# A fused transformer block: start, modulation, softmax helpers and the hand-over to the feed-forward rearranged

## The chip, the cores and the metric

The kernel runs on one core of a Trainium2 chip. The metric is the device time of one execution in microseconds (us), median of several runs; lower is better. The names of the engines in the profile are PE (TensorE, matrix multiplication), PEld (its weight loads), DVE (VectorE), ACT (ScalarE), POOL (GpSimd) and SP (SyncE, which issues most transfers here). A profile's span is about 1.7 us shorter than the time of the same run (493.4 against 495.09 us before).

## The reference

The input has 2048 tokens of 576 features, 32 heads of 18, and a feed-forward of 4608. Cut to what matters:

```python
mod = (silu(c) @ w_mod)             # six vectors of 576: sa, ca, ga, sb, cb, gb
h = layernorm(x) * (1 + ca) + sa
q, k, v = h @ wqkv
phi(q) = [softmax(q w_phi), softmax(-q w_phi)]    # per head; the same for k
kv = sum over tokens of phi(k) v ;  z = sum of phi(k)
x = x + ga * ((phi(q) kv / (phi(q) z)) @ wo)
h = layernorm(x) * (1 + cb) + sb
x = x + gb * (relu(h @ w1) @ w2)
```

`kv` sums over all tokens, so the whole key and value pass must end before the first attention output. That gives the kernel three parts: the key/value loop over 16 tiles of 128 tokens, a transition (two tiles of attention output must be ready before the feed-forward can start), and the feed-forward in five blocks, with the other 14 tiles' attention output interleaved.

## The kernel before

The parts that the argument touches. Instructions of the loop are placed by a scheduler from data dependences and priorities; in the last part PE's order is that of the program.

```python
# start: one transfer per weight; fold W_k with w_phi; the 60 one-column modulation matmuls
load_rows(nc.sync, wk_raw, A_wqkv[:, D:2 * D], False)
...
def mod_columns(parts, dst):                 # 2 x 30 matmuls whose moving operand has ONE column
    ps = one()
    ...     nc.tensor.matmul(ps[p0:p0 + pn, n * NC + ci:n * NC + ci + 1],
                             lhsT=wmod_sb[i][0:k, ck, ci * P:ci * P + pn], rhs=siluc[0:k, ck:ck + 1], ...)

def k_softmax(t):                            # one half on GpSimd, the other on DVE
    nc.vector.tensor_reduce(out=R[:, 0, :], in_=E, axis=AXX, op=ALU.add)
    nc.scalar.activation(out=R[:, 0, :], in_=R[:, 0, :], func=ACT.Ln)
    nc.scalar.activation(out=R[:, 1, :], in_=R[:, 0, :], func=ACT.Exp, scale=-1.0)
    for sgn, eng in ((1, nc.gpsimd), (0, nc.vector)):
        e = E[:, sgn * H:(sgn + 1) * H, :]
        eng.tensor_tensor(out=e, in0=e, in1=R[...].to_broadcast([P, H, DH]), op=ALU.mult)

def a_filler(t):                             # extra work of loop step t
    if t == 0: fold_transposes(wq_raw, wqT, "a")
    if t == 1: fold(wqT, wq_sb, "a")
    if t == 3:
        nc.gpsimd.tensor_copy(rep[:], ...)
        mod_row(2, ga_row)                   # a row: 10 matmuls of 288 columns
    if t == 5:
        mod_row(5, gb_row); mod_columns((3, 4), mod2)
    if 7 <= t < 13: q_part(...)              # query pieces
    if t == 14:
        for ci in range(NC):
            nc.gpsimd.tensor_tensor(out=wo_sb[:, ci, :], in0=wo_sb[:, ci, :], in1=ga_row[:], op=ALU.mult)

# transition
num_tile(0); q_part(3, 0); q_part(3, 1); num_tile(1); tr_tile(0); q_part(3, 2)
wo_tile(0); tr_tile(1); wo_tile(1); feat(0, ...)   # then the feed-forward's first block
```

`num_tile` is numerator, denominator and their quotient; its last step adds two halves (`o_sb`) on GpSimd. `tr_tile` transposes it, `wo_tile` is the output projection with the residual and the second norm.

The softmax here doesn't subtract the row's maximum and nothing guards it: scores larger than these inputs give would overflow.

## Time and profile before

| stage of the profiled run | from to (us) | length |
|---|---|---|
| start, to the end of the first key tile | 0 to 27.1 | 27.1 |
| loop, to the end of the last kv tile | 27.1 to 120.1 | 93.0 |
| kv to kvzd (the masked kv) | 120.1 to 121.9 | 1.8 |
| transition | 121.9 to 142.6 | 20.7 |
| feed-forward, first block | 142.6 to 199.0 | 56.4 |
| feed-forward, the rest | 199.0 to 493.4 | 294.4 |

Median time 493.17 us. The table by stage of the kernel before: stretch in us, its length, busy us (and instructions) of each engine, PE's granted clock as a share, DMA share and GB/s.

```profile
27.10:53.00 25.90, 24.19 (x221) 15.93 (x219) 21.70 (x49) 21.29 (x57) 9.75 (x7) 0.93 0.09 29
53.00:119.40 66.40, 63.26 (x515) 39.57 (x514) 29.85 (x33) 43.83 (x103) 21.46 (x15) 0.92 0.29 102
121.90:142.60 20.70, 13.67 (x89) 7.64 (x89) 10.50 (x32) 8.77 (x25) 2.80 (x2) 0.80 0.22 78
142.60:198.90 56.30, 53.09 (x455) 36.91 (x454) 29.24 (x89) 15.49 (x46) 5.64 (x4) 0.95 0.09 27
198.90:449.70 250.80, 250.68 (x1726) 146.63 (x1724) 108.76 (x261) 52.56 (x120) 14.34 (x10) 1.00 0.02 8
```

From 198.9 to 449.7 us PE is busy 250.68 of 250.8 us, at a granted clock of 1.00. In front of that, the last rows show where it is not: in the transition PE works 13.67 of 20.7 us, at a mean clock of 0.80.

The waits of PE in the kernel before: who waited for whom, us in total, times, longest.

```profile
PE two L230 <- DMA rW<-in_A_wqkv_dram: 6.2, 1, 6.2
PE pt L512 <- POOL o_sb L506: 5.9, 4, 2.7
...
PE two L206 <- ACT rH L309: 2.7, 1, 2.7
PE two L230 <- DVE rW L237: 1.7, 1, 1.7
```

The first line is the start: PE waits for the key weights. `pt L512 <- POOL o_sb` is a tile's transposes waiting for the GpSimd addition, 2.7 us in the transition and 3.2 us in the first block. The third line is the loop's one long gap. The timeline of PE around it (start, us, engine, line, operation, operands, count, idle time in front and what ended it):

```profile
58.76 2.66 PE L206 MATMUL two<-rW,rep 128*128 128x288 bf16 x10 [2.75 <-ACT rH L309]
61.36 3.73 PE L195 MATMUL one<-siluc,rW 128*128 128x1 bf16 x50
65.01 2.10 PE L294 MATMUL two<-rW,rH 128*128 128x288 bf16 x8
...
67.40 2.06 PE L294 MATMUL two<-rW,rH 128*128 128x252 bf16 x8
```

Eight matmuls of 288 columns take 2.10 us there, 0.26 us each; at full clock they take 1.15 us. So the gap is followed by about 10 us near half speed: the granted clock was 0.52 from 58.76 to 68.0 us, where it was 1.00 from 35 to 58. What DVE and GpSimd did just ahead of the gap, two timelines of the kernel before:

```profile
49.01 6.91 POOL L409 TENSOR_TENSOR wo_sb<-wo_sb,ga_row 128x576 bf16<-128x576 bf16 x5
```

```profile
49.58 1.23 DVE L262 SCALAR_TENSOR_TENSOR rs<-mv,rs 128x2 f32<-128x2 f32 x1
50.73 5.35 DVE L266 TENSOR_SCALAR xn<-x_sb,rs 128x576 bf16<-128x576 bf16 x4
56.00 1.34 DVE L323 TENSOR_REDUCE R_sb<-rH 128x64 f32<-128x1152 bf16 x1
```

The scaling of `wo_sb` was written for step 14 of the loop, but nothing held it there, and the scheduler put it where GpSimd was free. DVE's normalisations (L266), about 0.4 us each otherwise, take 1.34 us each on average meanwhile, and the tiny instruction at 49.58 takes 1.23 us. The softmax of the tile behind them (L323) starts late.

### The profile page before, as it was taken

How to read it: one execution, taken by the hardware profiler on the slowest of the kernel's cores; microseconds unless marked ns; L12 is line 12 of the kernel's file. 1: busy time of each engine (PE TensorE's matmuls, PEld its weight loads, DVE VectorE, ACT ScalarE, POOL GpSimd, SP SyncE). 2: the span in 40 equal slices, each digit the busy share in tenths (PEclk: the TensorE clock that was granted, in tenths of full speed). 3: DMA queues.
4: the chain of work that ended last, by engine and by line, in shares of the span. 5: the costliest groups of instructions: out<-in, count | busy, mean ns of one | idle time of the engine just before them, and what ended most of it. 6: DMA issues, size and time to landing. Idle time of an engine off the chain costs nothing.

```text
span 493.4 us, 8203 instructions
## 1 busy us (share of the span) xinstructions
PE 464.2 (94%) x3490; PEld 289.8 (59%) x3490; DVE 227.9 (46%) x544; ACT 160.4 (33%) x391; POOL 59.5 (12%) x67
## 2 busy tenths in 40 slices
PE   3999799999679889999999999999999999999996
PEld 3756476565346567433677743467773337777674
DVE  5378833435545754233565432356443332453321
ACT  3369447886523312123211222321112220112300
POOL 4013622233201120000112000011100000110000
PEclk9989869999959999999999999999999999999999
DMA  8940065007200300000000000000000000000000
GB/s 256 362 129 1 1 248 185 1 1 241 84 1 1 108 1 13 13 0 0 2 14 13 13 12 1 0 1 14 13 12 13 0 1 2 23 14 13 1 1 25
DMA packets 17263, 22.67 MB, mean 46 GB/s; under 512 B 1994, under 2 KB 16586, under 8 KB 16714
## 3 DMA queue, kind: packets, MB, share of 16 engines
q1 hardware_dynamic: 16016, 22.12, 13.1%
q8 instruction: 27, 0.44, 0.4%
q10 hardware_dynamic: 1210, 0.02, 0.1%
q14 instruction: 10, 0.08, 0.1%
HBM read 19.78 MB, written 2.36 MB: 45 GB/s over the span
## 4 chain that ended last, share of the span: by engine, by line
PE 84%; DVE 6%; ACT 5%; POOL 1%; DMA 1%; issue 1%; SPq 0%; POOLq 0%; DVEq 0%; ACTq 0%
PE psf L569 29%; PE psf L549 25%; PE two L294 6%; PE psf L553 5%; PE psf L294 3%; PE num L469 2%; PE two L361 2%; PE one L195 2%; PE kvacc L337 1%; PE two L298 1%; POOL o_sb L506 1%; DMA x_sb<-in_A_x_dram 1%; PE pt L512 1%; ACT rH L285 1%; ACT rH L309 1%; PE psf L277 1%
## 5 line engine op out<-in xcount | busy, mean ns | idle before, releaser
L549 PE MATMUL psf<-h2T,rW 128*128 128x512 bf16 (+1 forms) x720 | 142.6, 341 | 0.0
L569 PEld LDWEIGHTS <-rH 128*128 128x128 bf16 x1152 | 109.8, 98 | 28.9 <-issue 0.7
L569 PE MATMUL psf<-rW,rH 128*128 128x288 bf16 x864 | 115.1, 286 | 0.0
L549 PEld LDWEIGHTS <-rW 128*128 128x128 bf16 x720 | 64.1, 99 | 57.3 <-issue 12.0
L559 DVE TENSOR_SCALAR rH<-psf 128x512 bf16<-128x512 f32 (+1 forms) x90 | 52.5, 583 | 97.2 <-PE psf L553 97.0
L557 ACT ACTIVATE rH<-psf 128x512 bf16<-128x512 f32 (+1 forms) x90 | 46.1, 512 | 129.7 <-PE psf L553 129.7
L506 POOL TENSOR_TENSOR o_sb<-rV 128x576 bf16<-128x576 f32 x16 | 22.8, 1424 | 296.2 <-DVE rV L502 296.2
L572 DVE TENSOR_TENSOR yt<-psf,gb_row 128x288 f32<-128x288 f32 x32 | 14.6, 455 | 63.7 <-PE psf L569 63.7
L294 PE MATMUL two<-rW,rH 128*128 128x288 bf16 (+2 forms) x256 | 43.0, 313 | 1.0 <-DVE rH L288 0.8
L569 PE MATMUL psf<-rEQ,rH 128*128 128x288 bf16 x288 | 40.5, 286 | 0.0
L323 DVE TENSOR_REDUCE R_sb<-rH 128x64 f32<-128x1152 bf16 x16 | 21.6, 1352 | 25.9 <-ACT rH L309 25.9
L328 POOL TENSOR_TENSOR rH<-rH,R_sb 128x576 bf16<-128x576 bf16 x16 | 24.3, 1521 | 74.7 <-ACT R_sb L325 66.9
L553 PE MATMUL psf<-h2T,rW 64*128 64x512 bf16 (+1 forms) x180 | 31.5, 346 | 0.0
L294 PEld LDWEIGHTS <-rH 128*128 128x128 bf16 x256 | 24.2, 104 | 11.7 <-issue 2.2
L515 ACT ACTIVATE oT<-pt 128x640 bf16<-128x640 bf16 x16 | 11.3, 709 | 57.5 <-PE pt L514 57.5
L553 PEld LDWEIGHTS <-rW 64*128 64x128 bf16 x180 | 8.6, 93 | 30.9 <-issue 30.9
L256 DVE BATCH_NORM_STATS2 st<-x_sb 128x6 f32<-128x288 bf16 x64 | 25.6, 438 | 2.2 <-DMA x_sb<-in_A_x_dram 2.2
L522 DVE TENSOR_TENSOR x_sb<-x_sb,psf 128x288 bf16<-128x288 bf16 x32 | 13.2, 450 | 22.4 <-PE psf L298 22.4
L309 ACT ACTIVATE rH<-two 128x576 bf16<-128x576 f32 x32 | 19.2, 657 | 8.6 <-PE two L298 8.5
L294 PE MATMUL psf<-wo_sb,oT 128*128 128x288 bf16 x128 | 19.3, 296 | 1.4 <-ACT oT L515 1.4
L266 DVE TENSOR_SCALAR xn<-x_sb,rs 128x576 bf16<-128x576 bf16 x32 | 16.7, 546 | 1.4 <-PE one L280 1.2
L260 ACT ACTIVATE rs<-mv,eps_t 128x1 f32<-128x1 f32 (+2 forms) x24 | 7.0, 297 | 31.7 <-DVE mv L257 31.7
(99 smaller groups left out, 407.1 us busy)
## 6 DMA issues: line engine op xcount, KB each, us to landing
rW<-in_B_w_dram SPq DMA_DIRECT2D x1, 4608.0 KB, 14.1
rW<-in_B_w_dram SPq DMA_DIRECT2D x3, 1296.0 KB, 9.4
rW<-in_w_mod_dram SPq DMA_DIRECT2D x6, 576.0 KB, 7.5
out_dram<-x_sb SPq DMA_DIRECT2D x16, 144.0 KB, 1.7
rW<-in_A_wqkv_dram SPq DMA_DIRECT2D x3, 576.0 KB, 5.3
rEQ<-in_B_w_dram SPq DMA_DIRECT2D x1, 1296.0 KB, 6.1
x_sb<-in_A_x_dram SPq DMA_DIRECT2D x1, 1152.0 KB, 10.7
x_sb<-in_A_x_dram SPq DMA_DIRECT2D x1, 576.0 KB, 6.6
```

Source lines behind the costliest of these rows:

```text
L256: nc.vector.bn_stats(out=s[:, hf, :], in_=x_sb[:, t, hf * HD2:(hf + 1) * HD2])
L266: nc.vector.tensor_scalar(out=xn[:, t % NX, :], in0=x_sb[:, t, :], scalar1=rs[:, n, t, 0:1], scalar2=rs[:, n, t, 1:2], op0=ALU.mult, op1=A ...
L294: nc.tensor.matmul(ps(bk)[:, 0:cn], lhsT=lhs(ci, 0, P), rhs=rhs[:, ci, c0:c0 + cn], start=(ci == 0), stop=False)
L309: nc.scalar.activation(out=E[:, sgn, :].rearrange("p (b f) -> p b f", b=2), in_=ps[:, :, 0:HD2], func=ACT.Exp, scale=1.0 - 2.0 * sgn)
L323: nc.vector.tensor_reduce(out=R[:, 0, :], in_=E, axis=AXX, op=ALU.add)
L328: eng.tensor_tensor(out=e, in0=e, in1=R[:, 1, sgn * H:(sgn + 1) * H].unsqueeze(2).to_broadcast([P, H, DH]), op=ALU.mult)
L506: nc.gpsimd.tensor_tensor(out=o_sb[:, t % NO, :], in0=tm[:, 0, :], in1=tm[:, 1, :], op=ALU.add)
L549: nc.tensor.matmul(hps[n][:, 0:nn], lhsT=w1a[:, ci, jj * P:(jj + 1) * P], rhs=h2T[:, ci, 0:nn], start=(ci == 0), stop=False)
L553: nc.tensor.matmul(hps[n][:, 0:nn], lhsT=w1b[b0:b0 + 64, j * P:(j + 1) * P], rhs=h2T[b0:b0 + 64, 4, 0:nn], start=False, stop=True)
L557: nc.scalar.activation(out=H1[:, jj, 0:nn], in_=hps[n][:, 0:nn], func=ACT.Relu)
L559: nc.vector.tensor_relu(H1[:, jj, 0:nn], hps[n][:, 0:nn])
L569: nc.tensor.matmul(ps[:, 0:cn], lhsT=H1[:, j, tt * P:(tt + 1) * P], rhs=w2q[j // 9][:, j % 9, c0:c0 + cn], start=(j == 0), stop=(j == NJ - 1))
```

## The change

The intent: use idle time of PE before the feed-forward, take waits out of the loop and the transition, and keep PE's clock up. The diff, cut to its core (helpers split into a matmul part and an evacuation part, memory moves, the order of later loads, the copy `rep` moved from GpSimd to DVE and a few evacuations moved between ACT and DVE are left out):

```diff
 # start
+    for k in range(NC):                        # five transfers instead of two
+        nc.sync.dma_start(wk_raw[0:n, k, :], A_wqkv[k * P:k * P + n, D:2 * D])
+    order.enter_context(tc.manual_schedule(engines=ALL3))   # PE, ACT, DVE in program order
+    warm = one()
+    for i in range(24):
+        nc.tensor.matmul(warm[:, 0:P], lhsT=ident[:, :], rhs=ident[:, :], start=True, stop=True)
     ...  fold before mod_columns((0, 1)); transposes chunk by chunk over all groups;
     ...  the first features in three PSUM banks instead of one
 # loop
-    softmax: Ln, Exp on ACT
+    if t < 5: Ln, Exp on ACT
+    else:     nc.vector.reciprocal(out=R[:, 1, :], in_=R[:, 0, :])
-    t == 5:  mod_row(5, gb_row); mod_columns((3, 4), mod2)
-    t == 14: wo_sb scaled on GpSimd
+    11 <= t < 16: wo_sb scaled on DVE
+    query pieces at t = 4, 5, 7, 8, 9, 11, 12, 13, 15
 # transition, in fixed order on PE, ACT and DVE, with two 3-bank PSUM buffers
+    modulation 3 and 4 as rows plus 12 one-column matmuls, 5 as a row, between the steps
+    first two tiles: the final addition on DVE; the residual added on PE (identity matmul)
+    wo_x_stats(0, xps[0]); ln_rstd(1, 0, 1); tr_mm(1, trp); tr_e(1, trp); ln_apply(1, 0) ...
 # feed-forward
-    a tile's steps every 5 slots
+    a tile's steps 6.5 us (first block) or 7.5 us apart; transposes 6.6 us after the numerator
```

## The prediction

> **What bounds the kernel now.** From 199 us on TensorE is busy 100% at full granted clock (table by stage): the feed-forward, whose matmuls the change leaves alone. Only the first 199 us can give anything. The timeline shows four losses there:
>
> - *Start.* TensorE waits 6.2 us for the key weights, then 1.7 us for a DVE copy queued behind layer-norm statistics (waits of PE). The first key tile ends at 27.1 us.
> - *Half-speed TensorE.* 288-column matmuls take 0.26 us each at 25 and 65 us, 0.13 later.[...] it is slow before 35 us, at 58.8 to 69.4 and at 142.6 to 148, each time after gaps or one-column matmuls.
> - *45 to 70 us.* GpSimd scales wo_sb for 6.91 us from 49.0; meanwhile four DVE normalisations take 5.35 us instead of about 1.5. The softmax behind them is late, PE idles 2.75 us at 56, then runs cold through a modulation row (2.66 us), 50 one-column modulation matmuls (3.7) and tile 6.[...]
> - *119 to 199 us.* kvzd is ready at 121.9, the feed-forward starts at 142.6: a serial chain over two tiles, PE busy 6.2 of the last 12.7 us. The first block then takes 56.4 us for some 51 of warm work: cold start about 2.6, waits for o_sb 3.2.
>
> **What the change does.**
>
> 1. Key weights arrive in five pieces, 24 dummy matmuls run before, order on PE, ACT, DVE is fixed, the fold precedes the modulation columns. First key tile ends near 21 us: 6 us gained.
> 2. Then to the last kv tile: warm work, summed from durations at 105 to 113 us (k and v 2.64 per tile, kv 0.6, query pieces 2.2/2.2/1.3, features 1.4 per block, folds 4, one row 1.3), is 77 us, plus 2.3 for an early query piece; I add 3 for cold clock, 4 for stalls: it ends near 107.5 (120.1 before). Wo scaling and a softmax reciprocal (estimate 0.56 us per tile, from 0.38 for 35 elements and 0.19 for 5) load DVE nearly like PE up to tile 11, but the GpSimd collision and 22 small ACT steps go.
> 3. The second norm's modulation becomes rows plus 12 tiny matmuls that fill gaps of the transition. kvzd to feed-forward: 20.7 to 18 us; its chain stays serial. The add moves from GpSimd (1.41) to DVE[...].
> 4. First block: warm clock, wider spacing: 56.4 to 52 us.
> 5. The rest, 294 us, unchanged. The second weight's load now waits into the transition; 3.9 MB took about 11 us, over 20 remain before use: no cost.
>
> Sum: 109 + 18 + 52 + 294 = **473 us**, range 465 to 481. Chances: faster by over 2% (below 483.3) 0.95, within 2% 0.045, slower 0.005. Start gives 6, loop 7, transition 3, first block 4.
>
> **Signs.** Right if: first key tile ends near 21 us; DVE normalisations stay near 0.4 us; no 2.7 us PE gap; feed-forward starts near 127 us with 0.13 us matmuls; no waits for o_sb in the first block.
>
> **What would make it wrong.** DVE as new bound in tiles 1 to 11 (PE waiting for DVE); TensorE cold for long after the 60 one-column matmuls at the start; the fixed ACT order in the transition, where the second tile's copy stands behind the first tile's square root; feed-forward weights late (PE waiting on a DMA).

## The result

The changed kernel took 478.02 us (median of 9 runs, 477.43 to 480.58), the kernel before 493.23 us (median of 15). The ratio is 0.9691, 95% interval 0.9672 to 0.971. All ratios here are the mean time of one kernel's fast runs over that of the other's fast runs of the same rounds, so not quite the ratio of the medians. All kernels below gave correct results.

| stage | before | predicted | after (profile) |
|---|---|---|---|
| start | 27.1 | 21 | 22.2 |
| loop | 93.0 | 86.5 | 89.6 |
| kv to kvzd | 1.8 | 1.5 | 1.8 |
| transition | 20.7 | 18 | 18.75 |
| first block | 56.4 | 52 | 51.5 |
| rest | 294.4 | 294 | 292.4 |
| span | 493.4 | 473 | 476.3 |

The prediction took its sum of stages for the time; the time is 1.75 us more than the span (478.05 for the profiled run).

The table by stage of the changed kernel, with its own stage borders:

```profile
22.20:53.00 30.80, 25.18 (x220) 15.94 (x220) 27.84 (x65) 19.41 (x55) 5.40 (x5) 0.94 0.37 102
53.00:111.60 58.60, 57.27 (x465) 35.41 (x464) 35.89 (x44) 40.44 (x81) 18.12 (x12) 1.00 0.23 86
113.60:132.30 18.70, 15.63 (x115) 8.53 (x116) 10.04 (x28) 9.74 (x29) 0.00 (x0) 0.91 0.02 2
132.30:183.90 51.60, 50.56 (x453) 36.30 (x453) 31.18 (x90) 15.20 (x45) 5.61 (x4) 1.00 0.32 107
183.90:433.40 249.50, 249.50 (x1726) 147.04 (x1724) 111.89 (x261) 52.53 (x120) 14.03 (x10) 1.00 0.02 8
```

The first stretch of the loop (22.2 to 53, the value of tile 0 to the start of tile 5) has PE busy only 25.18 of 30.8 us; the second 57.27 of 58.6. The first block runs at full clock with 1 us idle. The waits of PE in the changed kernel, the longest:

```profile
PE kvacc L373 <- DVE rH L364: 2.1, 4, 0.9
...
PE two L271 <- ACT rH L275: 1.6, 1, 1.6
PE n L327 <- ACT oT L608: 1.5, 1, 1.5
PE two L271 <- ACT rW L261: 0.9, 1, 0.9
```

The old long waits are gone, for the transfer, for `o_sb` in the feed-forward and for the tile after the gap. In their place stand PE waiting for DVE's softmax multiplication (L364), for ACT's copies of the folded weights (L271), and for the copy of the second tile in the transition (`n L327 <- ACT oT`). The timeline of PE at that last wait:

```profile
122.18 1.15 PE L327 MATMUL n<-wo_sb,oT 128*128 128x288 bf16 x8
...
126.48 1.76 PE L327 MATMUL n<-wo_sb,oT 128*128 128x288 bf16 x8 [1.50 <-ACT oT L608]
...
128.53 2.45 PE L219 MATMUL n<-rW,rep 128*128 128x288 bf16 x10
...
132.78 1.16 PE L665 MATMUL psf<-h2T,rW 128*128 128x256 bf16 x7 [0.18 <-DVE h2T L318]
```

The same projection takes 1.15 us for the first tile and 1.76 us for the second, after the wait; the row behind it takes 2.45 us (1.71 earlier in the transition). The granted clock was 0.61 from 126.4 to 128.5 us and 0.50 from 128.5 to 130.0, and 1.00 from 113.6 to 126.4. Whether the wait did that is taken up in experiment 7.

### The profile page after: what moved, and what is told of

It is laid out like the page before. It is cut to its first block, busy times and chain, and to the rows that moved or that the text cites. A ratio compares the mean times of both kernels' runs of the same rounds, so it can differ in the third digit from the quotient of the medians.

```text
span 476.3 us, 8229 instructions
## 1 busy us (share of the span) xinstructions
PE 458.4 (96%) x3490; PEld 288.5 (61%) x3490; DVE 243.1 (51%) x563; ACT 155.8 (33%) x372; POOL 48.0 (10%) x59
## 4 chain that ended last, share of the span: by engine, by line
PE 72%; DVE 1%; ACT 0%; issue 0%
PE psf L683 30%; PE psf L665 28%; PE psf L669 5%; PE psf L327 3%; PE num L542 2%; PE psf L331 1%; PE psf L304 1%; PE pt L603 1%; PE pt L605 1%; PE n L219 1%; PE n L327 0%; PE psf L307 0%; ACT h2T L315 0%; DVE x_sb L687 0%; DVE x_sb L633 0%; DVE yt L686 0%
## 5 line engine op out<-in xcount | busy, mean ns | idle before, releaser
L665 PE MATMUL psf<-h2T,rW 128*128 128x512 bf16 (+1 forms) x720 | 140.5, 338 | 0.5 <-ACT h2T L315 0.2
L683 PEld LDWEIGHTS <-rH 128*128 128x128 bf16 x1152 | 109.1, 98 | 29.7 <-issue 0.7
L683 PE MATMUL psf<-rW,rH 128*128 128x288 bf16 x864 | 116.9, 286 | 0.0
L587 POOL TENSOR_TENSOR o_sb<-rV 128x576 bf16<-128x576 f32 x14 | 19.6, 1403 | 286.8 <-DVE rV L583 286.8
L327 PE MATMUL two<-rW,rH 128*128 128x288 bf16 (+2 forms) x256 | 40.2, 295 | 1.9 <-DVE rH L277 0.6
L364 POOL TENSOR_TENSOR rH<-rH,R_sb 128x576 bf16<-128x576 bf16 x16 | 23.5, 1472 | 78.5 <-ACT R_sb L359 38.8
L327 PEld LDWEIGHTS <-rH 128*128 128x128 bf16 x256 | 23.0, 100 | 12.3 <-issue 3.8
L282 DVE BATCH_NORM_STATS2 st<-x_sb 128x6 f32<-128x288 bf16 x60 | 24.2, 438 | 2.0 <-DMA x_sb<-in_A_x_dram 2.0
L411 ACT ACTIVATE rEQ<-two 126x512 bf16<-126x512 f32 (+1 forms) x34 | 17.7, 600 | 11.6 <-PE two L403 11.6
L608 ACT ACTIVATE oT<-pt 128x640 bf16<-128x640 bf16 x14 | 9.8, 703 | 32.4 <-PE pt L605 32.4
L364 DVE TENSOR_TENSOR rH<-rH,R_sb 128x576 bf16<-128x576 bf16 x16 | 17.5, 1096 | 0.7
L398 PE MATMUL two<-rH 128*126 128x512 bf16 (+1 forms) x68 | 16.5, 382 | 0.6 <-ACT rH L342 0.6
```

The lines of the kernel that those rows point to most:

```text
L282: nc.vector.bn_stats(out=s[:, hf, :], in_=x_sb[:, t, hf * HD2:(hf + 1) * HD2])
L327: nc.tensor.matmul(ps(bk)[:, 0:cn], lhsT=lhs(ci, 0, P), rhs=rhs[:, ci, c0:c0 + cn], start=(first and ci == 0), stop=False)
L364: eng.tensor_tensor(out=e, in0=e, in1=R[:, 1, sgn * H:(sgn + 1) * H].unsqueeze(2).to_broadcast([P, H, DH]), op=ALU.mult)
L411: nc.scalar.activation(out=Eq[b][0:nf, g, sgn, :], in_=pss[k][0:nf, :], func=ACT.Exp, scale=1.0 - 2.0 * sgn)
L587: adder.tensor_tensor(out=o_sb[:, t % NO, :], in0=tm[:, 0, :], in1=tm[:, 1, :], op=ALU.add)
L665: nc.tensor.matmul(hps[n][:, 0:nn], lhsT=w1a[:, ci, jj * P:(jj + 1) * P], rhs=h2T[:, ci, 0:nn], start=(ci == 0), stop=False)
```

## The experiments

Twelve kernels ran, each for three rounds beside the kernel before; three groups of four, each group on one chip. The medians of the kernel before in them were 492.68, 493.08 and 492.61 us.

### 1. wo_sb scaled on DVE, nothing else (kernel before)

```diff
-        if t == 14:
-            for ci in range(NC):
-                nc.gpsimd.tensor_tensor(out=wo_sb[:, ci, :], in0=wo_sb[:, ci, :], in1=ga_row[:], op=ALU.mult)
+        if 11 <= t < 16:
+            nc.vector.tensor_tensor(out=wo_sb[:, t - 11, :], in0=wo_sb[:, t - 11, :], in1=ga_row[:], op=ALU.mult)
```

> The kernel before, with one thing changed: the five multiplications that scale wo_sb run on DVE (as in the changed kernel) instead of GpSimd. Theory A (collision): the 6.91 us of GpSimd work at 49 us held up four DVE normalisations (5.35 us instead of about 1.5) and so made the 2.75 us PE gap at 56 us and the cold clock after it. Then the normalisations come back to about 0.4 us each, the gap at 56 us goes, matmuls of the sixth tile run at 0.13 us, and the time falls by 4 to 7 us (ratio 0.986 to 0.992). Rival B: PE is slowed there by the 60 one-column modulation matmuls, not by the gap. Then the time falls by at most 2.5 us and the tile after the one-column matmuls still runs at 0.26 us per matmul.

Measured: 487.72 us, ratio 0.9886 (0.9852 to 0.992). Theory A holds. The timelines of DVE and of PE in this run:

```profile
47.67 0.15 DVE L262 SCALAR_TENSOR_TENSOR rs<-mv,rs 128x2 f32<-128x2 f32 x1
...
48.35 1.45 DVE L266 TENSOR_SCALAR xn<-x_sb,rs 128x576 bf16<-128x576 bf16 x4 [0.16 <-PE one L280]
49.71 1.56 DVE L408 TENSOR_TENSOR wo_sb<-wo_sb,ga_row 128x576 bf16<-128x576 bf16 x4
```

```profile
53.81 1.70 PE L206 MATMUL two<-rW,rep 128*128 128x288 bf16 x10
55.44 3.39 PE L195 MATMUL one<-siluc,rW 128*128 128x1 bf16 x53
...
60.08 2.06 PE L294 MATMUL two<-rW,rH 128*128 128x252 bf16 x8
```

The four normalisations take 1.45 us together, the tiny instruction 0.15, the five scalings 0.45 and 1.56. No gap stands ahead of the row, which now takes 1.70 us instead of 2.66. One part of A was wrong: the value tile after the one-column matmuls still runs at about half speed for a while (2.06 us at 60.08, where eight such matmuls take 1.15 at 52.46). That led to experiment 6.

### 2. The softmax multiplication wholly on DVE (changed kernel)

```diff
-        for sgn, eng in ((1, nc.gpsimd), (0, nc.vector)):
+        for sgn, eng in ((1, nc.vector), (0, nc.vector)):
```

> The changed kernel, with the key softmax's multiplication run wholly on DVE (both signs) instead of half on GpSimd. Theory A: DVE and GpSimd serialise on these operands anyway (a DVE half takes 0.75 us alone and about 1.7 us when GpSimd started first), so the split buys nothing: both halves on DVE take about 1.5 us, kv waits shrink in tiles 1 to 5 (PE waited 2.1 us for that multiplication), and the time falls by 1 to 4 us against the changed kernel (ratio to the kernel before 0.961 to 0.967). Rival B: DVE is the fuller engine in tiles 1 to 11, and 0.75 us more per tile on it makes the loop slower: 2 to 8 us more than the changed kernel (ratio 0.973 to 0.985).

Measured: 475.24 us, ratio 0.9635 (0.9598 to 0.9671), against 0.9691 for the changed kernel. Theory A. DVE did more work, and the loop got shorter: 86.1 us (21.8 to 107.9) instead of 89.6 (22.2 to 111.8), and 3.3 of these 3.5 us are there when tile 5 starts (49.4 instead of 53.0). The line of the table by stage for that stretch in experiment 2:

```profile
21.79:49.37 27.58, 23.79 (x218) 15.45 (x219) 26.46 (x64) 19.23 (x53) 0.00 (x0) 1.00 0.44 122
```

PE's idle time in the whole loop fell from 6.9 to 4.7 us. The other 1.2 us is PE's busy time: the changed kernel's profile has a spell at half speed at 34 to 38 us (granted clock 0.50 from 35.5 to 37.5; eight matmuls at 35.52 take 2.10 us), which is missing here. Experiment 7, with the changed kernel's loop, does not have it either (1.15 us for the same eight, behind the same gap of 1.55 us), and its loop takes 88.1 us. So the spell is not the collision's, and about 2 us of loop are shown for the split, near the 2.8 us between the medians.

Why the split costs, the instances of L364 in the changed kernel show, from its timelines of GpSimd and DVE; first a pair where GpSimd started first:

```profile
26.99 1.16 POOL L364 TENSOR_TENSOR rH<-rH,R_sb 128x576 bf16<-128x576 bf16 x1 [18.17 <-ACT R_sb L359]
```

```profile
27.06 1.70 DVE L364 TENSOR_TENSOR rH<-rH,R_sb 128x576 bf16<-128x576 bf16 x1
```

and one where DVE did:

```profile
58.45 0.76 DVE L364 TENSOR_TENSOR rH<-rH,R_sb 128x576 bf16<-128x576 bf16 x1
```

```profile
58.59 1.64 POOL L364 TENSOR_TENSOR rH<-rH,R_sb 128x576 bf16<-128x576 bf16 x1 [4.59 <-DVE R_sb L361]
```

A half takes 0.75 us on DVE and 1.16 us on GpSimd when alone. When the two meet, the one that starts first keeps its time in these pairs, and the other takes longer: 1.70 us on DVE, or 1.64 us on GpSimd. The pair lasts about 1.8 us either way. Both halves on DVE last less, in experiment 2's timeline of DVE:

```profile
54.82 1.43 DVE L364 TENSOR_TENSOR rH<-rH,R_sb 128x576 bf16<-128x576 bf16 x2
```

The traces show it in both directions, with the numbers above; by what mechanism the second instruction is held up, they do not show. The normalisations that experiment 1 set free are a case of it on other operands: 1.34 us each beside GpSimd's scaling in the kernel before, 0.36 us each in experiment 1 (1.45 us for four).

### 3. No dummy matmuls (changed kernel)

```diff
-    for i in range(24):
-        nc.tensor.matmul(warm[:, 0:P], lhsT=ident[:, :], rhs=ident[:, :], start=True, stop=True)
```

> The changed kernel without the 24 dummy matmuls at the start. Theory A: they only warm the clock for the start; without them TensorE stays at half speed past 20 us, the first key tile ends 1 to 3 us later than 22.2 us, total 1 to 3 us more than the changed kernel (ratio 0.971 to 0.975). Rival B: the one-column modulation matmuls at 12.5 to 16.8 us let the clock fall again anyway, so the dummies do nothing: the same time within 0.5 us (ratio 0.968 to 0.970).

Measured: 478.0 us, ratio 0.9688 (0.9655 to 0.9721), the same as with them. Rival B's number holds. In both profiles the first ten fold matmuls take 1.33 us and the 60 one-column matmuls 4.36 us, so the 24 dummies (2.74 us) did not make the start faster. That the one-column matmuls undo the warming was not shown: PE is at the same slow rate in front of them. The dummies are not without effect: in six of the eight profiled kernels that have them (not in the changed kernel's profile) the transposes behind them speed up, from 0.69 to 0.44 us for four, between 4.8 and 7.2 us. But in the five of these six that keep the start's order the 60 one-column matmuls take 4.36 us again, so the higher speed did not last.

### 4. Only the spacing in the feed-forward (kernel before)

```diff
-            step = 5 ; put(k, num_tile, t) ; put(k + 4, tr_tile, t) ; put(k + 5, wo_tile, t)
+            gap = 6.5 if b == 0 else 7.5
+            put(us, num_tile, t0 + i) ; put(us + 6.6, tr_tile, t0 + i) ; put(us + 8.3, wo_tile, t0 + i)
```

> The kernel before, with only the changed kernel's spacing of the attention steps inside the feed-forward. Theory A: the 3.2 us of PE waits for o_sb in the first block go, and nothing else: time falls by 2.5 to 4 us (ratio 0.992 to 0.995), first block from 56.4 to about 53 us. Rival B: the waits only move to another place (transposes and features later in the block): less than 1 us.

Measured: 489.02 us, ratio 0.9906 (0.9876 to 0.9936). Theory A, a little larger than said. The first block took 52.25 us (141.67 to 193.92) instead of 56.4, and PE's waits for `o_sb` in it are gone; one wait of 0.7 us for a normalisation appeared. A part is not spacing: full speed came back after the block's first pair of matmul groups here (eight matmuls took 2.07 us, then 1.18 and 1.04), after more than two in the kernel before (2.07, 1.89, 1.37, then 1.05). Without the numerator between them, the first four pairs took 6.04 us here and 7.18 in the kernel before; in experiments 1 and 12, with the old spacing, the block took 55.3 and 55.4 us. So about 1 us of the 4.2 is the clock and about 3 us the spacing. From the last first-layer matmuls of one block to the first of the next, the last two such stretches also shortened, from 48.2 to 47.8 and from 43.4 to 43.0 us, as in the changed kernel.

### 5. Logarithm and exponential back on ACT (changed kernel)

```diff
-        if t < 5:
+        if t < NT:
```

> The changed kernel with one part undone: the softmax reciprocal of tiles 5 to 15 is again logarithm and exponential on ACT instead of one DVE instruction (0.55 us, measured in the changed kernel's trace). Theory A: ACT has room and the DVE instruction only shortened the softmax's chain, which PE does not wait for in those tiles: within 1 us of the changed kernel (ratio 0.967 to 0.971). Rival B: the loop leans on the short chain, and PE waits again: 2 to 4 us slower (ratio 0.973 to 0.977). Rival C: DVE was too full, and freeing 6.1 us on it makes it faster by over 1 us (below 0.967).

Measured: 477.84 us, ratio 0.9697 (0.9667 to 0.9727). Theory A: this part of the change gives nothing that can be measured.

### 6. The second norm's modulation as rows (experiment 1's kernel)

```diff
-            mod_columns((3, 4), mod2)
+            mod_row(3, o_sb[:, 0, :]); mod_row(4, o_sb[:, 1, :])
+            ... 12 matmuls: lhsT=o_sb[:, n, ci * P:ci * P + pn], rhs=ident[:, 0:1]
```

> The first experiment (the kernel before with wo_sb scaled on DVE), and in addition the second norm's modulation as two rows of 288-column matmuls and 12 one-column matmuls in place of 60 one-column matmuls, at the same place of the loop. Theory A: the 60 one-column matmuls (3.4 us) both cost PE time and let the clock fall (the value tile after them ran at 0.26 us per matmul), so rows (1.3 us each) plus 12 small ones (0.7) gain 0.5 to 1 us of PE time and 1 to 2 us of clock: 1.5 to 3 us less than the first experiment (487.7), ratio 0.982 to 0.986. Rival B: the count of PE time is all, the clock dips for other reasons: 0 to 0.7 us less.

Measured: 488.41 us, ratio 0.9914 (0.9888 to 0.9941), not better than experiment 1 (0.9886). The timeline of PE:

```profile
55.13 4.99 PE L206 MATMUL two<-rW,rep 128*128 128x288 bf16 x30
60.05 0.38 PE L410 MATMUL one<-ident,o_sb 128*128 128x1 bf16 x6
...
61.98 1.16 PE L295 MATMUL two<-rW,rH 128*128 128x252 bf16 x8
```

Both theories missed in part. The value tile did stay at full speed, 1.16 us where experiment 1 had 2.06. That is one trace each, and half speed differs between profiles elsewhere, so chance is not ruled out. But three rows take 4.99 us, 1.66 us each and not 1.3, so rows and small matmuls together cost 5.7 us where one row and 60 one-column matmuls cost 5.6 (1.70, 3.39 and 0.48 for seven earlier ones). As work, the new form of the modulation is not cheaper; its worth in the change is that it can stand where PE would idle.

### 7. The second tile's copy first (changed kernel)

```diff
+    trp = one_a(); tr_mm(1, trp); tr_e(1, trp)
     wo_x_stats(0, xps[0])
     ln_rstd(1, 0, 1)
-    trp = one_a(); tr_mm(1, trp); tr_e(1, trp)
     ln_apply(1, 0)
```

> The changed kernel with one move in the fixed order of the transition: the second tile's transposes and their ACT copy stand ahead of the first tile's statistics, square root and residual copy. Theory A: in the changed kernel PE waited 1.5 us for that copy and then ran the projection and a modulation row at half clock (1.76 and 2.45 us instead of 1.15 and 1.3); with the copy first the wait falls below 0.7 us, the clock stays full, and the feed-forward starts 1.5 to 3 us earlier after kvzd (18.75 us now): ratio 0.963 to 0.966. Rival B: the chain of the first tile's statistics is as long, and only PE idle time moves: within 0.5 us of the changed kernel.

Measured: 475.97 us, ratio 0.9666 (0.9629 to 0.9702). The interval overlaps with the changed kernel's, but the trace is plain: kvzd to feed-forward took 17.0 us (113.27 to 130.26) instead of 18.75. The timeline of PE:

```profile
125.11 1.15 PE L327 MATMUL n<-wo_sb,oT 128*128 128x288 bf16 x8 [0.45 <-ACT oT L608]
...
126.42 1.71 PE L219 MATMUL n<-rW,rep 128*128 128x288 bf16 x10
```

The wait fell from 1.50 to 0.45 us, and the projection and the row run at full clock. The numbers are Theory A's, but its claim about the clock is not shown. Experiment 10 (and 9, with the same durations to 0.01 us) has the changed kernel's order and its wait of 1.50 us, and there full clock held:

```profile
126.69 1.16 PE L327 MATMUL n<-wo_sb,oT 128*128 128x288 bf16 x8 [1.50 <-ACT oT L607]
...
128.01 1.71 PE L219 MATMUL n<-rW,rep 128*128 128x288 bf16 x10
```

From kvzd to the feed-forward both took 18.0 us. So the new order is worth about 1.0 us of the 1.8; the other 0.7 us is a half-speed spell that this wait does not always bring. In experiments 9 and 10 it came later, on the first matmuls of the feed-forward (1.55 and 1.68 us for seven, 1.16 in the changed kernel).

### 8. Experiments 2 and 7 together

```diff
-        for sgn, eng in ((1, nc.gpsimd), (0, nc.vector)):
+        for sgn, eng in ((1, nc.vector), (0, nc.vector)):
     ...
+    trp = one_a(); tr_mm(1, trp); tr_e(1, trp)
     wo_x_stats(0, xps[0])
     ln_rstd(1, 0, 1)
-    trp = one_a(); tr_mm(1, trp); tr_e(1, trp)
```

> The changed kernel with the second experiment's softmax multiplication on DVE and the seventh's order in the transition together. If both gains are independent (one in the loop, one in the transition) they add: 475.2 less 1.5 to 3 us, ratio 0.957 to 0.961. If they are not, it equals the better of the two.

Measured: 472.08 us, ratio 0.9579 (0.9557 to 0.9601). The gains add, or a little more: the span is 470.0 us, 6.3 less than the changed kernel's, against 3.6 and 2.0 for the two alone. This version beats both kernels.

### 9. The key weights in one large transfer (changed kernel)

```diff
-    for k in range(NC):
-        n = P if k < 4 else 64
-        nc.sync.dma_start(wk_raw[0:n, k, :], A_wqkv[k * P:k * P + n, D:2 * D])
+    load_rows(nc.sync, wk_raw, A_wqkv[:, D:2 * D], False)
```

> The changed kernel with the key weights loaded as in the kernel before (one large transfer and one small one, not five). Theory A: the pieces let the transposes start at 4.2 us instead of 6.2 us, and they are the start's gain: the first key tile ends 1.5 to 2 us later than 22.2 us, total 1.5 to 2 us more (ratio 0.972 to 0.974). Rival B: the transposes at half clock catch up, or the later fold waits for something else: under 0.7 us.

Measured: 480.09 us, ratio 0.9725 (0.9676 to 0.9775). The first transposes of experiment 9:

```profile
7.15 0.44 PE L251 MATMUL two<-ident,rW 128*126 128x128 bf16 x4 [2.77 <-DMA rW<-in_A_wqkv_dram]
```

They start at 7.15 us, where the changed kernel's start at 4.30, and the first key tile ends at 25.0 instead of 22.2. Theory A: the pieces are worth about 2 us of the time (2.1 between the medians; the intervals of the two ratios overlap). The start's end is not exact: in six profiles with the changed start as it is, it lies between 21.0 and 23.4 us, and the key tile's nine matmuls of 288 columns take 1.41 us in experiment 2, 1.54 in the changed kernel and 2.28 here, so some of the 2.8 us may be that.

### 10. The start's order left to the scheduler (changed kernel)

```diff
     order = ExitStack()
-    order.enter_context(tc.manual_schedule(engines=ALL3))
     warm = one()
```

> The changed kernel with the fixed order of PE, ACT and DVE at the start given back to the scheduler (which puts most of the one-column modulation matmuls between the folds again). Theory A: the fixed order is what took the waits for copies and the late fold out of the start: the first key tile ends 1 to 3 us later than 22.2 us (ratio 0.971 to 0.975). Rival B: with the pieces and the transposes over all groups in place, the order does not matter: within 0.7 us.

Measured: 479.36 us, ratio 0.971 (0.9668 to 0.9751). The first key tile ends at 25.4, 3.2 us later than with the fixed order: PE stood 4.74 us at 7.4 waiting for a normalisation whose transposes the scheduler had put ahead of the folds. Only 1.3 us of it is left in the median. So Theory A by its numbers, at the low end, with a ratio whose interval overlaps the changed kernel's. The trace's loss was larger than the total's. About 0.7 us of it is half speed in the key tile itself (2.28 us for nine matmuls that take 1.54 in the changed kernel), which differs between profiles of the same start; where the loop gave the rest back was not traced.

### 11. Experiment 8 with logarithm and exponential on ACT

```diff
-        if t < 5:
+        if t < NT:
```

> The eighth experiment (both improvements) with logarithm and exponential on ACT in place of the DVE reciprocal. Theory A: with the whole softmax multiplication on DVE, DVE has become the full engine of tiles 5 to 11, and 0.55 us less per tile there helps: 0.5 to 2 us faster than 472.1 (ratio 0.954 to 0.957). Rival B: PE is not held by DVE there, and the longer chain over ACT costs: the same or up to 2 us slower (ratio 0.957 to 0.962).

Measured: 472.88 us, ratio 0.9586 (0.954 to 0.9632). No gain: Rival B. With both halves of the softmax on it DVE still does not hold PE enough for 0.55 us per tile to matter.

### 12. The softmax multiplication wholly on DVE in the kernel before

```diff
-        for sgn, eng in ((1, nc.gpsimd), (0, nc.vector)):
+        for sgn, eng in ((1, nc.vector), (0, nc.vector)):
```

> The kernel before with the softmax multiplication wholly on DVE, the second experiment's edit without the rest of the change. Theory A: DVE had more slack there and in 11 of 16 tiles started ahead of GpSimd, so the collision on the softmax cost PE under 1 us: ratio 0.997 to 1.003. It was the change that made it cost more, by filling DVE so that GpSimd starts first in the first four tiles. Rival B: the collision cost was always there: 2.5 to 4 us faster (ratio 0.992 to 0.995).

Measured: 494.43 us, ratio 1.0014 (0.997 to 1.0058). The number is Theory A's, but the reason is not shown. The same edit freed GpSimd, and the scaling of `wo_sb` moved forward, from 49.01 to 45.27 us, and took 7.36 us instead of 6.91; meanwhile two softmax multiplications took 3.11 us on DVE, which take 1.42 at 43.58, and two normalisations 2.67, which take 0.74 at 53.02. The timelines of GpSimd and PE:

```profile
45.27 7.36 POOL L409 TENSOR_TENSOR wo_sb<-wo_sb,ga_row 128x576 bf16<-128x576 bf16 x5 [33.22 <-ACT ga_row L209]
```

```profile
57.01 2.89 PE L206 MATMUL two<-rW,rep 128*128 128x288 bf16 x10 [4.52 <-ACT rH L309]
```

The gap grew from 2.75 to 4.52 us, while PE's waits for the softmax multiplication, 0.9 us in total before, were gone. Two collisions traded places. Experiment 1, where only the softmax's collision is left, has 1.2 us of PE waits for that multiplication, and the changed kernel 2.1 us. A clean test would have had both edits in the kernel before; it was not run, so whether the softmax's collision was made worse by the change or was only hidden before stays open.

## Why the prediction was right

- **The start, 6 us predicted, 4.9 measured: right in kind.** The pieces are worth about 2 us (experiment 9) and the fixed order perhaps 1.3 us of total time (experiment 10), both with overlapping intervals. The dummy matmuls, which the prediction listed without a price, are worth nothing (experiment 3: 478.0 us without them, 478.02 with them). Slow matmuls had no price in the prediction either: in the changed kernel PE is busy 11.49 us from 10 to 22 us, and 16 matmuls of 128 columns at 16.79 us still take 1.89 us, where eight take 0.61 us at 42.85. Whether the one-column matmuls among that work are the reason was not tested.
- **The collision of GpSimd and DVE: right.** Experiment 1 alone gave 5.0 us. DVE's normalisations are at 0.42 us in the changed loop, and no gap of 2.7 us is left.
- **The loop, 93.0 to 86.5 predicted, 89.6 measured: the term that was mis-sized.** The step was "I add 3 for cold clock, 4 for stalls". PE idled 6.9 us in the loop, not 4: 5.6 us between 22.2 and 53 and 1.3 us after (length less busy time in the table by stage). Work and cold clock together came out as forecast: 82.6 us busy against 79.3 and 3. That is partly luck, for the work was larger (81.2 us in experiment 7's loop, without the half-speed spell) and the cold clock cost less. Most of the idle time sits in the first five tiles, and experiment 2 returned 2.3 us of it by taking away one thing: DVE and GpSimd meeting in the softmax. The prediction had this collision in hand for the scaling of `wo_sb` and did not apply it to the instruction pair that meets in almost every tile. The named risk "DVE as new bound in tiles 1 to 11" is half right: PE did wait for DVE, but its half took 1.50 to 1.72 us where GpSimd had started first and 0.75 alone, and in experiment 2 more work on DVE made the loop shorter.
- **"22 small ACT steps go" was counted as a help in the loop.** Experiments 5 and 11 show no gain from it.
- **The modulation, "one row 1.3": mis-sized.** A row takes 1.66 to 1.71 us at full clock. As a replacement of one-column matmuls it gave nothing (experiment 6); what was right is that it fills gaps of the transition.
- **The transition, 18 predicted, 18.75 measured.** The named risk came true: the second tile's copy stood behind the first tile's square root. It cost about 1.0 us of waiting (experiment 7 against 9 and 10), which the sum did not contain as a term; the other 0.7 us of the trace's 1.8 is a half-speed spell that the order is not shown to cause.
- **First block, 52 predicted, 51.5 measured: right.** Granted clock 1.00 in the block and no waits for `o_sb`. Experiment 4 got 4.2 us there in the kernel before, about 3 by the spacing and about 1 from an earlier return of the clock. That the changed kernel's first matmuls were at full clock is in part chance: experiments 9 and 10 had them slower (1.55 and 1.68 us for seven, against 1.16). The named risk of late feed-forward weights did not come: PE never waited for a transfer there.
- **The rest, 294 predicted, 292.4 measured.** Two parts. The spacing shortens each block by some 0.4 us (seen in experiment 4 too); why, with no PE wait in either trace, is not known. After the last block's first layer the changed kernel and its variants end 0.8 us sooner than the kernel before and its variants; this was not followed up. The prediction said "unchanged", so these 2 us are luck: without them the time would have been about 480 us, near the end of the range.
- **The sign "feed-forward starts near 127 us" failed**: it starts at 132.3, by 1.2 us from the start, 3.1 from the loop, 0.3 from kvzd and 0.75 from the transition. These and the 1.75 us between span and time, less 2.1 us from the feed-forward, make up the 5 us between 473 and 478.02.

## What to carry to other kernels

Before work is split between GpSimd and DVE, look at one meeting in the trace: here both halves of an elementwise product took 1.43 us on DVE alone and about 1.8 us when split, and 6.91 us of work on GpSimd that nothing waited for held up a chain that PE then waited 2.75 us for. Where a scheduler places instructions, an instruction written late in the program may run early on an idle engine, so read its place from the timeline and not from the source. In a fixed order, put the copy that PE waits for ahead of steps that wait for another engine's statistics: that one move took 1.0 us off PE's wait here. And before a half-speed stretch is put down to the wait in front of it, look at the same wait in other profiles: here the same gap of 1.50 us was followed by a projection of 1.76 us in one, at a granted clock of 0.61, and of 1.16 us in others.
